# Sorted attention and routed experts on one core: tokens kept on chip and gathered by GpSimd

## The chip, the cores and the metric

The kernel runs on one core of one Trainium2 chip. Times are device microseconds (us). Five engines matter: PE (TensorE, matmuls; its weight loads are recorded as PEld and overlap it), DVE (VectorE), ACT (ScalarE), POOL (GpSimd) and SP (SyncE, which here only issues transfers); DMA moves data between DRAM and the core's memory. "Clock" is the share of TensorE's full clock that was granted in a stretch. L415 is line 415 of the kernel's file.

Every median below is of runs on the chip. A ratio is the mean time of one kernel's fast runs over that of the other's fast runs of the same rounds, so it is not quite the ratio of the medians quoted.

## The reference

```python
# q, k, v: (4, 8, 768, 64) float32; sort_net: (4, 8, 8, 8); 3072 tokens of 512; 8 experts
P = sort_net
for _ in range(5):                          # soft permutation of 8 blocks per head
    P = exp(P - rowmax(P)); P /= rowsum(P); P /= colsum(P)
k_sorted[i] = sum_j P[i, j] * k_block[j]    # blocks of 96 rows; the same for v
attn  = softmax(q_block @ k_sorted_block.T / 8)     # inside each block of 96
x     = (attn @ v_sorted_block) as (3072 tokens, 512 = 8 heads * 64)
for e in range(8):                          # each token has one expert, domain_id
    out[domain_id == e] = relu(x[domain_id == e] @ w1[e]) @ w2[e]   # w1 512x1024, w2 1024x512
```

In the data drawn here the experts get 354 to 420 tokens each.

## The kernel before

It works in three stages. The setup makes the permutation and a table from slots to tokens, which goes through DRAM in 24 scatters (they run on beside attention until 150 us). Attention runs per half of the batch: K and V are mixed over the blocks by matmuls, copied, transposed by more matmuls, copied again; q is transposed; then come scores, exponential, product with V, and a division.

```python
for n in range(12):                                   # mix over blocks
    nc.tensor.matmul(mix_ps, PTg, Ka16[:, n * 512:(n + 1) * 512], start=True, stop=True)
    nc.scalar.copy(Ks16[:, n * 512:(n + 1) * 512], mix_ps)
    # ... the same for V, copied by VectorE
for n in range(24):                                   # then transpose, 4 columns of blocks at a time
    for cc in range(4):
        nc.tensor.transpose(tps[0:64, cc * 128:(cc + 1) * 128], Ks16_v[:, c0 + cc, :], idf16)
    pcopy(n, kTs[:, c0 * 128:(c0 + 4) * 128], tps[0:64, :])
# ... the same for V; then per head:
nc.tensor.matmul(sc_ps[:, ii * 96:(ii + 1) * 96], kTs_v[:, m, :],      # kTs_v: step of 128 elements
                 qT_h_v[:, :, i0 + ii, :], start=True, stop=True)
# ...
nc.sync.dma_start(x_dram...., x_g....)                # x to DRAM, once per half of the batch
```

The experts take 512 slots each. Weights are loaded two experts deep, the rows of x are fetched from DRAM by their indices, transposed, multiplied, and the results scattered.

```python
for e in range(8):
    w1e = wpool.tile([128, 4096], FP16, tag="w1e")    # wpool: bufs=2
    # ... w2e; both loaded from GpSimd's queue
    for tcc in range(4):                              # fetch 128 rows of x
        nc.gpsimd.indirect_dma_start(X[:, tcc * 512:(tcc + 1) * 512], None, x_dram.ap(), ...)
    # ... 16 transposes of X into xT, copied
    for fc in range(8):
        for dc in range(4):
            nc.tensor.matmul(h_ps, w1e[...], xT[:, dc * 512:(dc + 1) * 512], ...)   # contiguous columns
        nc.scalar.activation(hT[:, fc * 512:(fc + 1) * 512], h_ps, func=AF.Relu)
    for tcc in range(4):
        # ... 8 matmuls into o_ps, copied to out_sb (2 buffers)
        nc.gpsimd.indirect_dma_start(out, ..., out_sb, None, ...)                    # scatter 128 rows
```

The softmax here doesn't subtract the row's maximum and nothing guards it: scores larger than these inputs give would overflow.

## Time and profile before

| | us |
|---|---|
| median before (438.42 to 439.76, 3 runs) | 438.49 |
| setup, until 31 us | 31 |
| attention, 31 to 222 | 191 |
| gap and experts, 222 to 437 | 215 |

The first view cuts the profile of the kernel before into stretches. The columns are: stretch, its length, the busy time of each engine with its instructions in brackets, the mean TensorE clock, the DMA share, and GB/s.

```profile
core 0: us, PE busy (x) PEld busy (x) DVE busy (x) ACT busy (x) POOL busy (x), PEclk, DMA share, GB/s
0.00:31.00 31.00, 1.95 (x6) 0.74 (x6) 9.89 (x62) 3.02 (x8) 5.28 (x19) 1.00 0.88 155
...
157.00:222.00 65.00, 58.38 (x368) 47.21 (x366) 27.56 (x98) 17.19 (x35) 0.00 (x0) 0.50 0.00 1
222.00:244.00 22.00, 0.58 (x2) 0.39 (x2) 0.86 (x4) 0.00 (x0) 8.86 (x10) 0.50 0.88 190
244.00:437.00 193.00, 138.48 (x640) 62.99 (x640) 16.46 (x32) 56.09 (x96) 70.29 (x71) 0.85 0.65 129
```

In 157–222, attention, PE is busy 58 of 65 us at half the clock: PE is the limit there. In 222–244 almost nothing computes. In 244–437 PE is busy for 138 of 193 us.

The second view is the list of waits of the kernel before: who waited, for what, the sum, how often, and the longest one.

```profile
DVE out_sb L42 <- DMA out_dram<-out_sb,s2tx: 92.9, 10, 11.9
...
POOL w1e L315 <- DMA x_dram<-x_g: 79.3, 1, 79.3
...
POOL out_dram L354 <- DMA out_dram<-out_sb,s2tx: 58.7, 16, 6.9
```

The one wait of 79.3 us explains the gap: the first load of weights waits until x has been written to DRAM (the pool of the weight tiles is opened only after attention's pools are closed), so no weight moves during attention. The other two are the scatters of results: only one is under way at a time, and the copies out of PSUM wait for their two buffers.

The third view is two lines of the groups of instructions of the kernel before: line, engine, operation, tiles, shapes, count, busy us, mean ns of one, idle time before them and its releaser.

```profile
L340 PE MATMUL h_ps<-xT,w1e 128*128 128x512 f16 x256 | 71.6, 444 | 2.4 <-ACT xT L44 2.0
...
L270 PE MATMUL sc_ps<-qT_h,kTs 64*96 64x96 f16 x256 | 49.2, 364 | 7.2 <-DVE qT_h L265 7.1
L270 PEld LDWEIGHTS <-kTs 64*96 64x96 f16 x256 | 44.3, 252 | 14.1 <-DVE qT_h L265 10.8
```

A score matmul is narrow (96 columns), yet its record lasts 364 ns, and that of its weight load, with a step of 128 elements, 252 ns. Records of matmuls overlap, so the mean of one is not its share of the time: 49.2 us for 256 is 192 ns each.

### The profile page before, as it was taken

The numbers are of one execution on the slowest core, as the hardware profiler recorded it, in microseconds if no ns is written. First come the engines' busy times: TensorE is split into PE (matmuls) and PEld (weight loads), VectorE is DVE, ScalarE is ACT, GpSimd is POOL, SyncE is SP. The second block draws the span as 40 slices with busy tenths as digits, with TensorE's granted clock in tenths as the row PEclk, the third lists the DMA queues.
The fourth block names the chain that finished last, engine by engine and source line by source line (L and its number), as shares of the span: only waits on it lengthen the run. The fifth ranks groups of instructions, "written<-read, shape, count | busy, mean of one in ns | idle before, by whom it ended". The sixth has DMA issues, their size and how long they took to land. (4 is left out here: it accounts for less than half of the span.)

```text
span 437.5 us, 4602 instructions
## 1 busy us (share of the span) xinstructions
PE 306.0 (70%) x1722; PEld 188.3 (43%) x1722; DVE 113.6 (26%) x367; ACT 126.7 (29%) x234; POOL 111.7 (26%) x128
## 2 busy tenths in 40 slices
PE   0109789999897389898920595959493966959680
PEld 0004476777676367676720242424241422424330
DVE  5306734454444234444420001010100001010110
ACT  2004743333225342222200232314141513323420
POOL 4001334331010100000007433426242624421211
PEclk9999955555557955555555597988898886969995
DMA  7950960000009100000049987877696876764110
GB/s 146 206 86 0 160 130 2 2 2 0 2 2 241 50 1 0 1 1 2 0 144 152 220 176 125 176 142 150 134 179 121 166 129 119 144 129 107 73 48 24
DMA packets 23921, 40.40 MB, mean 92 GB/s; under 512 B 3706, under 2 KB 15996, under 8 KB 23708
## 3 DMA queue, kind: packets, MB, share of 16 engines
q0 software_dynamic: 22688, 36.87, 44.5%
q1 hardware_dynamic: 1212, 3.26, 2.2%
q8 instruction: 13, 0.21, 0.2%
q14 instruction: 8, 0.07, 0.0%
HBM read 56.69 MB, written 11.60 MB: 156 GB/s over the span
## 5 line engine op out<-in xcount | busy, mean ns | idle before, releaser
L340 PE MATMUL h_ps<-xT,w1e 128*128 128x512 f16 x256 | 71.6, 444 | 2.4 <-ACT xT L44 2.0
L348 PE MATMUL o_ps<-w2e,hT 128*128 128x512 f16 x256 | 59.2, 387 | 4.6 <-ACT out_sb L44 4.6
L354 POOL DMA_INDIRECT out_dram<-out_sb,s2tx x32 | 32.0, 1002 | 103.8 <-DMA out_dram<-out_sb,s2tx 58.7
L270 PE MATMUL sc_ps<-qT_h,kTs 64*96 64x96 f16 x256 | 49.2, 364 | 7.2 <-DVE qT_h L265 7.1
L275 ACT ACTIVATE ET<-sc_ps 96x384 f16<-96x384 f32 x64 | 31.1, 486 | 79.4 <-PE sc_ps L270 79.4
L42 DVE COPY out_sb<-o_ps 128x512 f32<-128x512 f32 x16 | 11.1, 692 | 160.9 <-DMA out_dram<-out_sb,s2tx 92.9
L333 PE MATMUL xps<-idf_118,X 128*128 128x128 f16 x128 | 13.4, 248 | 56.3 <-DVE xT L42 34.1
L270 PEld LDWEIGHTS <-kTs 64*96 64x96 f16 x256 | 44.3, 252 | 14.1 <-DVE qT_h L265 10.8
L216 POOL DMA_INDIRECT slot2tok<-val_239,dest_i x24 | 23.9, 994 | 87.9 <-DMA slot2tok<-val_239,dest_i 53.9
L340 PEld LDWEIGHTS <-w1e 128*128 128x128 f16 x256 | 28.4, 113 | 40.3 <-issue 20.3
L344 ACT ACTIVATE hT<-h_ps 128x512 f16<-128x512 f32 x64 | 38.1, 597 | 21.9 <-PE h_ps L340 21.5
L348 PEld LDWEIGHTS <-hT 128*128 128x128 f16 x256 | 25.3, 99 | 36.8 <-issue 8.1
L279 PE MATMUL av_ps<-VsC,ET 96*96 96x65 f16 x256 | 39.7, 296 | 0.0
L321 POOL DMA_INDIRECT X<-x_dram,s2tx x32 | 32.8, 1025 | 18.6 <-issue 8.8
L333 PEld LDWEIGHTS <-X 128*128 128x128 f16 x128 | 9.7, 108 | 61.4 <-issue 36.7
L279 PEld LDWEIGHTS <-ET 96*96 96x96 f16 x256 | 30.3, 177 | 10.0 <-issue 9.2
L264 PE MATMUL qps<-idf_118,Qa_133 128*64 128x128 f16 x192 | 33.4, 313 | 0.4 <-ACT VsC L44 0.4
L44 ACT COPY xT<-xps 128x512 f16<-128x512 f16 x16 | 9.4, 586 | 79.3 <-PE xps L333 79.3
L265 DVE COPY qT_h<-qps 64x384 f16<-64x384 f16 x64 | 21.8, 341 | 33.1 <-PE sc_ps L270 30.4
L315 POOL DMA_DIRECT2D w1e<-in_moe_w_dram x8 | 6.7, 832 | 79.9 <-DMA x_dram<-x_g 79.3
L44 ACT COPY out_sb<-o_ps 128x512 f32<-128x512 f32 x16 | 9.4, 585 | 49.4 <-DMA out_dram<-out_sb,s2tx 43.7
L264 PEld LDWEIGHTS <-Qa_133 128*64 128x64 f16 x192 | 18.5, 152 | 8.7 <-issue 3.2
(276 smaller groups left out, 246.0 us busy)
## 6 DMA issues: line engine op xcount, KB each, us to landing
w1e<-in_moe_w_dram POOLq DMA_DIRECT2D x8, 1024.0 KB
w2e<-in_moe_w_dram POOLq DMA_DIRECT2D x8, 1024.0 KB
Ka_126<-in_k_dram POOLq DMA_DIRECT2D x4, 768.0 KB
Va_127<-in_v_dram POOLq DMA_DIRECT2D x4, 768.0 KB
Qa_133<-in_q_dram POOLq DMA_DIRECT2D x2, 1536.0 KB
x_dram<-x_g SPq DMA_DIRECT2D x2, 1536.0 KB
X<-x_dram,s2tx POOLq DMA_INDIRECT x32
out_dram<-out_sb,s2tx POOLq DMA_INDIRECT x32
```

Source lines behind the costliest of these rows:

```text
L216: nc.gpsimd.indirect_dma_start(slot2tok.ap(), bass.IndirectOffsetOnAxis(ap=dest_i[:, j:j + 1], axis=0), val2[:, 2 * j:2 * j + 2], None, bo ...
L264: nc.tensor.transpose(qps[0:64, t * 128:(t + 1) * 128], q16[:, (t0 + t) * 64:(t0 + t + 1) * 64], idf16)
L265: nc.vector.tensor_copy(qT_h[:, t0 * 128:(t0 + 3) * 128], qps[0:64, 0:384])
L270: nc.tensor.matmul(sc_ps[:, ii * 96:(ii + 1) * 96], kTs_v[:, m, :], qT_h_v[:, :, i0 + ii, :], start=True, stop=True)
L275: nc.scalar.activation(ET, sc_ps, func=AF.Exp, scale=0.125)
L279: nc.tensor.matmul(av_ps[:, ii * 65:(ii + 1) * 65], ET[:, ii * 96:(ii + 1) * 96], VsC_v[:, m, :], start=True, stop=True)
L321: nc.gpsimd.indirect_dma_start(X[:, tcc * 512:(tcc + 1) * 512], None, x_dram.ap(), bass.IndirectOffsetOnAxis(ap=s2tx[:, 8 * e + 2 * tcc + ...
L333: nc.tensor.transpose(xps[:, tcc * 128:(tcc + 1) * 128], X[:, tcc * 512 + dc * 128:tcc * 512 + dc * 128 + 128], idf16)
L340: nc.tensor.matmul(h_ps, w1e[:, dc * 1024 + fc * 128: dc * 1024 + fc * 128 + 128], xT[:, dc * 512:(dc + 1) * 512], start=(dc == 0), stop=( ...
L344: nc.scalar.activation(hT[:, fc * 512:(fc + 1) * 512], h_ps, func=AF.Relu)
L348: nc.tensor.matmul(o_ps, hT[:, fc * 512 + tcc * 128: fc * 512 + tcc * 128 + 128], w2e[:, fc * 512:(fc + 1) * 512], start=(fc == 0), stop=( ...
L354: nc.gpsimd.indirect_dma_start(out, bass.IndirectOffsetOnAxis(ap=s2tx[:, 8 * e + 2 * tcc:8 * e + 2 * tcc + 1], axis=0), out_sb, None, boun ...
```

## The change

The intent: one matmul both mixes and transposes a piece of K or V (its moving operand is a mask times the permutation). x never leaves the chip: it is kept transposed, with the four 128-wide chunks of one token side by side (`xT[p, token, 4]`), and GpSimd gathers the tokens of an expert from it with `indirect_copy`. An expert has 448 slots; a loop with a count read at run time takes what exceeds them, which here is nothing, so it runs zero times. Weight tiles go from two to five, and five experts' weights are loaded during attention. The 64 slots beyond 384 of two neighbouring experts share one tile ("tails"), so there are 28 scatters where there were 32. The order of instructions on PE, ACT, DVE and GpSimd is that of the program.

The diff is a rewrite; this is its core, with cuts marked.

```diff
-    P_dram, x_dram, slot2tok, cnt_rt, base_rt = ...            # four tables and x through DRAM
+    wpool = ctx.enter_context(tc.tile_pool(name="wp", bufs=5))
+    xT = keep.tile([128, NTOK, 4], FP16, tag="xT")             # x, on chip
 ...
-            nc.tensor.matmul(mix_ps, PTg, Ka16[:, n * 512:(n + 1) * 512], ...)   # mix, copy,
-            nc.tensor.transpose(tps[0:64, ...], Ks16_v[:, c0 + cc, :], idf16)    # transpose, copy
+    def interleave(p):                                          # GpSimd orders K, V, q of two heads
+        nc.gpsimd.tensor_copy(kv[:, :, 0::3, :], ks[:, h].rearrange("p h (t d) -> p t h d", d=D))
+        # ... two more
+    def kv_mm(p, lst):                                          # mixes and transposes at once
+        # ...
+            nc.tensor.matmul(o[:, s]..., kv[:, t, h], M[:, bh]..., start=True, stop=True)
 ...
-                nc.sync.dma_start(x_dram..., x_g...)
+    def x_tr(p):                                                # 8 transposes, then into xT
+        # ...
+        nc.scalar.copy(xT[:, b * 768:(b + 1) * 768, hp], o.rearrange("p i c -> p (i c)"))
 ...
+            if 6 <= p <= 14 and p % 2 == 0:
+                load_w((p - 6) // 2)                            # five experts during attention
 ...
-                nc.gpsimd.indirect_dma_start(X[...], None, x_dram.ap(), ...)      # 4 per expert
-                ... nc.tensor.transpose(xps[...], X[...], idf16) ...
+    def gather(e):
+        xg = moe.tile([128, CAP, 4], FP16, tag="xg", name="xg")
+        for s in range(2):
+            nc.gpsimd.indirect_copy(xg[:, s * 224:(s + 1) * 224, :], xT, gidx[:, e, s * 14:(s + 1) * 14], ...)
 ...
-                nc.tensor.matmul(h_ps, w1e[...], xT[:, dc * 512:(dc + 1) * 512], ...)
+                nc.tensor.matmul(h_ps, w1e[:, dc, fc * 128:(fc + 1) * 128], xg[:, :, dc], ...)  # step of 4
 ...
+        for e in range(NE):
+            if first and e >= 1 and e + 4 < NE:
+                load_w(e + 4)                                   # experts 5, 6, 7
+            ...
+            hts[e] = up(e, xg)
+            xg = gather(e + 1)
+            down(e, hts[e])                                     # 3 x (8 matmuls, copy, scatter)
+            if e % 2 == 1:
+                tails(e - 1, hts[e - 1], hts[e])
```

## The prediction

> **What bounds it now.** The table of stages (busy time per stretch) shows three stages. 0–31 us: setup, PE busy 2 us. 31–222: attention. PE is busy 58.4 of the 65 us in 157–222 at granted clock 0.50, with narrow matmuls: by groups, a score matmul is 364 ns and its strided weight load 252 ns; the timeline shows eight scores in 1.54 us. 222–437: experts. The list of waits shows one wait of 79.3 us of the first weight load on the write of x to DRAM, so weights start only then; PE idles 21.5 us for the first gathered X. In 244–437 PE is busy 138 of 193 us although 32 matmuls at full clock take 7.1 us (about 221 ns each): outputs wait for scatters (DVE 92.9 us, ACT 43.7, GpSimd 58.7). The chain of waits is nearly empty and no help.
>
> **Start, estimated 32 us.** No bounce of tables through 24 scatters; but the new mask products and one-hot tables stand on DVE ahead of the first K/V copies.
>
> **Attention, estimated 98 us (now 191).** Mixing and transposing become one matmul; 640 separate mixing/transposing matmuls and their copies, and 64-to-96-column strided weight loads, go. Per pair of heads DVE now has, costed by like shapes in the trace: 512-element fp32 copy 0.68, half of it 0.42, 768-element copy about 0.55, two V copies 0.84, four reciprocals and products 2.35: 4.85 us. ACT: 0.59+0.39+4×0.49+0.79 = 3.7. PE: 74 matmuls, about 4 us at full clock, 5.5–6 at half. So about 6 us, DVE-bound, PE near it, times 16, plus the last transpose: attention ends near 130 us. Weights of five experts load meanwhile.
>
> **Experts, estimated 190 us (now 215).** PE needs only 12–13 us per expert at full clock. The new limit is GpSimd, one in-order queue. Each expert has two gathers of 224 entries. No such instruction is in this trace. [...] Scatters still wait for each other (the order of instructions shows each waiting for the previous one's semaphore): 1.0 us issue plus about 2.5 us landing in the trace: 28 cost about 75 us of that same queue. Also, the load of the sixth and eighth expert's second weights waits for the 64-row tails of the pair before, ahead of the next gather: some 10 us. Thus about 200 us; I shade this to 190 as gathers may be quicker.
>
> **Total 320 us**, 80% range 258–360. Faster by over 2%: 0.96; within 2%: 0.015; slower: 0.025.
>
> **Right or wrong in the profile.** Right: gathers 5–7 us each; GpSimd busy or waiting for scatters almost throughout the expert stage; PE idle before the up matmuls, released by GpSimd; PE busy about 100 us there; gaps largest at experts 3 and 5; attention about 6 us per pair with DVE over 75% busy; the first weights landed before attention ends. Wrong: gathers near 1–2 us make experts PE-bound, about 115 us, total near 245; pairs of 7–8 us mean that in-order waits, or GpSimd's interleaving copies, bind attention.
>
> **What would make it wrong.** The gather's time above all: each microsecond moves the total by 16. [...] Then: scatters landing slower next to weight loads; [...] a PE clock staying at half in attention; strided moving operands from the gathered x.

The sum for the experts came to about 200 us, shaded to 190, and the total to 320; the 75 us of scatters and the 10 us of waits do not make up the 200. The gather of 5–7 us is the author's estimate. PE's figures are estimates too. The numbers of the kernel before to set beside them: 32 matmuls of 512 columns take 7.07 us at a clock of 1.00 (from 255.57 us), and a transpose of 128 columns adds 58 ns at 1.00 (L248: four in 0.38 us, eight in 0.61) and 108 ns at 0.50 (L254: 0.58 and 1.01).

## The result, and the profile after

The kernel after takes 400.25 us (median of 4 runs, 399.19 to 400.75), against 439.12 us (4 runs, 438.42 to 440.33) of the kernel before in the same rounds; the ratio is 0.9107, with a 95% interval of 0.9081 to 0.9134. It is faster, as predicted, but 80 us slower than the predicted 320 and outside the range of 258 to 360.

The stretches of the kernel after, with the same columns as above (38 is the start of the first scores, 136 the end of attention's matmuls, 153 the first up matmul of the first expert):

```profile
0.00:38.00 38.00, 5.91 (x74) 5.42 (x76) 32.84 (x87) 3.52 (x8) 24.16 (x39) 1.00 1.08 158
38.00:136.00 98.00, 79.05 (x1153) 68.49 (x1147) 69.67 (x210) 68.16 (x110) 38.94 (x49) 0.62 0.89 145
136.00:153.00 17.00, 0.00 (x0) 0.10 (x1) 0.00 (x0) 0.37 (x1) 1.75 (x2) 0.50 0.00 0
153.00:399.00 246.00, 151.33 (x512) 52.13 (x511) 19.37 (x28) 34.84 (x64) 50.92 (x49) 0.81 0.23 52
```

| stage | before, us | predicted, us | after, us |
|---|---|---|---|
| start | 31 | 32 | 38 |
| attention | 191 | 98 | 98 |
| experts to the end | 215 | 190 | 263 |

So attention gave back the 93 us that it should, and the experts took 48 us more than before instead of 25 us less. In the expert stage no engine looks busy: PE 151 of 246 us, GpSimd 51, the DMA share 0.23. Something serial that the busy times do not show must bound it.

Three groups of the kernel after:

```profile
L415 PE MATMUL h_ps<-xg,w1e 128*128 128x448 f16 x256 | 102.6, 574 | 98.7 <-POOL xg L405 98.7
...
L405 POOL INDIRECT_COPY xg<-xT,gidx 128x896 f16 x16 | 19.2, 1203 | 143.7 <-issue 143.7
...
L431 PE MATMUL o_ps<-w2e,hT 128*128 128x512 f16 x192 | 42.9, 380 | 0.0
```

The gather seems cheap, 1203 ns each. But GpSimd is idle 143.7 us before the sixteen gathers, put down to "issue", that is, to nothing that the profile shows; and PE waits 98.7 us for them. GpSimd's timeline of the kernel after shows why (start, length, engine, line, operation, count, and in brackets the idle time before it with its releaser):

```profile
143.91 1.19 POOL L405 INDIRECT_COPY xg<-xT,gidx 128x896 f16 x1 [33.48 <-issue]
152.44 1.19 POOL L405 INDIRECT_COPY xg<-xT,gidx 128x896 f16 x1 [7.34 <-issue]
160.96 1.19 POOL L405 INDIRECT_COPY xg<-xT,gidx 128x896 f16 x1 [7.32 <-issue]
169.47 1.19 POOL L405 INDIRECT_COPY xg<-xT,gidx 128x896 f16 x1 [7.32 <-issue]
170.85 1.12 POOL L423 DMA_INDIRECT out_dram<-o_sb,sidx  x1 [0.19 <-DVE o_sb L422]
174.51 1.02 POOL L423 DMA_INDIRECT out_dram<-o_sb,sidx  x1 [2.54 <-issue]
178.07 0.97 POOL L423 DMA_INDIRECT out_dram<-o_sb,sidx  x1 [2.54 <-issue]
179.04 0.84 POOL L355 DMA_DIRECT2D w1e<-in_moe_w_dram  x1
191.69 0.93 POOL L356 DMA_DIRECT2D w2e<-in_moe_w_dram  x1 [11.81 <-PE o_ps L438]
200.01 1.22 POOL L405 INDIRECT_COPY xg<-xT,gidx 128x896 f16 x1 [7.39 <-issue]
```

Gathers that follow each other start 8.51 to 8.53 us apart. The second one's record ends at 152.44 + 1.19 = 153.63, and PE's first up matmul starts at 153.69; after a load of weights that ends at 192.62 the next gather's record ends at 201.23, 8.61 us later. So a gather takes about 8.5 us and only its last 1.2 us is recorded; the "idle" time is the gather at work. This is how the trace reads, 1.2 us recorded and 8.5 us of spacing; half_entries below tests it.

The same lines show the rest of the queue: 2.5 us between two scatters, and a wait of 11.81 us in front of the second load of expert 5, for matmuls of L438, which are the tails. The list of waits of the kernel after has it twice:

```profile
POOL w2e L356 <- PE o_ps L438: 22.8, 2, 11.8
```

And PE's timeline of the kernel after shows the up matmuls:

```profile
153.69 12.83 PE L415 MATMUL h_ps<-xg,w1e 128*128 128x448 f16 x32 [19.21 <-POOL xg L405]
166.34 5.36 PE L431 MATMUL o_ps<-w2e,hT 128*128 128x512 f16 x24
```

Thirty-two up matmuls of 448 columns take 12.83 us, 401 ns each; 24 down matmuls of 512 columns take 5.36 us, 223 ns each (the 574 and 380 ns of the groups are records that overlap). The narrower one is nearly twice as slow. The difference between the two is how the moving operand lies: `xg[:, :, dc]` has a step of 4 elements (8 bytes), `w2e[:, fc]` is contiguous. All eight up stages take 12.83 us, while the mean clock in them lies between 0.78 and 1.00.

Summed over GpSimd's timeline, from 136.6 us (the end of the first gather, 145.10, less 8.53) to the end at 398.7:

| what stands in GpSimd's queue | us |
|---|---|
| 16 gathers of 8.53 | 136.5 |
| scatters of experts 0 to 6, each waiting for the one before | 71.3 |
| waits of the sixth and eighth experts' loads for the tails | 22.8 |
| issuing loads | 5.3 |
| expert 7 after its gather: matmuls, four scatters, the end (less the scatters of expert 6) | 26 |
| sum | 262 |

The sum is the length of the stage, 262 us. That is a reading, not yet a test.

### The profile page after: what moved, and what is told of

The parts are those of the page before. It is cut to its first block, busy times and chain, and to the rows that moved or that the text cites. A ratio compares the mean times of both kernels' runs of the same rounds, so it can differ in the third digit from the quotient of the medians.

```text
span 398.7 us, 4513 instructions
## 1 busy us (share of the span) xinstructions
PE 236.3 (59%) x1732; PEld 126.1 (32%) x1732; DVE 121.9 (31%) x324; ACT 106.9 (27%) x182; POOL 115.8 (29%) x138
## 5 line engine op out<-in xcount | busy, mean ns | idle before, releaser
L415 PE MATMUL h_ps<-xg,w1e 128*128 128x448 f16 x256 | 102.6, 574 | 98.7 <-POOL xg L405 98.7
L417 ACT ACTIVATE hT<-h_ps 128x448 f16<-128x448 f32 x64 | 34.8, 544 | 206.9 <-PE h_ps L415 206.9
L422 DVE COPY o_sb<-o_ps 128x512 f32<-128x512 f32 x28 | 19.4, 692 | 232.0 <-PE o_ps L431 227.3
L405 POOL INDIRECT_COPY xg<-xT,gidx 128x896 f16 x16 | 19.2, 1203 | 143.7 <-issue 143.7
L423 POOL DMA_INDIRECT out_dram<-o_sb,sidx x28 | 28.1, 1005 | 62.5 <-DMA out_dram<-o_sb,sidx 28.8
L348 ACT COPY xT<-x_ps 128x768 f16<-128x768 f16 x16 | 29.9, 1867 | 10.5 <-PE x_ps L347 10.3
L340 DVE TENSOR_TENSOR xr<-av_ps,rc 96x256 f16<-96x256 f32 x64 | 26.9, 421 | 2.2
L277 PE MATMUL kv_ps<-M,kvx 128*128 128x128 f16 x192 | 24.2, 291 | 4.9 <-DVE M L125 4.9
L277 PEld LDWEIGHTS <-kvx 128*128 128x128 f16 x192 | 17.3, 132 | 6.8 <-issue 4.9
L356 POOL DMA_DIRECT2D w2e<-in_moe_w_dram x8 | 7.3, 908 | 22.8 <-PE o_ps L438 22.8
L313 PE MATMUL v_ps<-idf_86,kvT_301 64*128 64x64 f16 x128 | 8.5, 221 | 7.4 <-ACT xT L348 7.4
L313 PE MATMUL v_ps<-idf_86,kvT_302 64*128 64x64 f16 x128 | 8.1, 219 | 7.6 <-ACT xT L348 7.6
```

The lines of the kernel that those rows point to most:

```text
L277: nc.tensor.matmul(o[:, s].rearrange("p i c -> p (i c)"), kv[:, t, h], M[:, bh].rearrange("p i c -> p (i c)"), start=True, stop=True)
L313: nc.tensor.transpose(o[:, i], kt[r, c0:c0 + 128], idf16[r, r])
L340: nc.vector.tensor_tensor(xr[p][:, 4 * ih:4 * ih + 4, h * D:(h + 1) * D], o[0:BLK, :, 0:D], rc.unsqueeze(2).to_broadcast([BLK, 4, D]), op= ...
L348: nc.scalar.copy(xT[:, b * 768:(b + 1) * 768, hp], o.rearrange("p i c -> p (i c)"))
L405: nc.gpsimd.indirect_copy(xg[:, s * 224:(s + 1) * 224, :], xT, gidx[:, e, s * 14:(s + 1) * 14], i_know_this_is_slow=True)
L415: nc.tensor.matmul(h_ps, w1e[:, dc, fc * 128:(fc + 1) * 128], xg[:, :, dc], start=(dc == 0), stop=(dc == 3))
```

## The experiments

The main theory, A: GpSimd's in-order queue bounds the expert stage, and its largest term is the gather, which costs by entry. Rivals: B, the gather costs by the bytes that it moves; C, PE bounds the stage, because the up matmuls run at half speed, and the gathers lie mostly under them; D, the scatters' landing or the loads that wait for the tails are the cause, and the gathers matter little. Each run below is an edit of the kernel after; five of the kernels are correct, and the others give a wrong result, as marked. Several were with the kernel before on the same chip; the ratios are to that kernel. One caution: edits of the expert stage alone also moved the start of the first gather, between 133.7 and 137.2 us (136.6 in the kernel after), for a reason that no run shows. So 2 or 3 us of any difference below may not come from the edit.

### half_entries: half the entries per gather

Wrong result: 111 of 224 entries are gathered, into two tiles that were zeroed once.

```diff
-            nc.gpsimd.indirect_copy(xg[:, s * 224:(s + 1) * 224, :], xT, ...)
+            nc.gpsimd.indirect_copy(xg[:, s * 224:s * 224 + 111, :], xT, ...)
```

> Wrong result on purpose: each gather fetches 111 entries in place of 224; everything else as in the changed kernel. Theory (the gather really takes the 8.5 us between starts, in proportion to its entries): the spacing of two gathers back to back falls to about 4.3 us; the GpSimd queue loses 16 x 4.2 = 67 us, PE becomes the limit, total 310 to 335 us. Rival (the 7.3 us of idle time before each gather record is a fixed cost of each instruction, or a wait): spacing stays near 8.5 us and the total near 400.

Measured: 340.92 us (2 runs), ratio 0.774 (0.770 to 0.778). GpSimd's timeline:

```profile
137.86 0.81 POOL L409 INDIRECT_COPY xg<-xT,gidx 128x444 f16 x1 [28.26 <-issue]
142.21 0.81 POOL L409 INDIRECT_COPY xg<-xT,gidx 128x444 f16 x1 [3.54 <-issue]
```

The spacing falls to 4.34 us, by 4.19 us for 113 entries: 37 ns per entry, which leaves about 0.2 us fixed. Removing 16 × 4.19 = 67 us from the queue removed 59 us from the kernel. The total lies a little above the expected 310 to 335, because the matmuls and their tails start to be waited for (the waits for tails are still 23.4 us). Theory A stands; C in its pure form falls, since PE's work is unchanged.

### half_elements: same entries, half the bytes

Wrong result: 224 entries of 2 elements.

```diff
-            nc.gpsimd.indirect_copy(xg[:, s * 224:(s + 1) * 224, :], xT, ...)
+            nc.gpsimd.indirect_copy(xg[:, s * 224:(s + 1) * 224, 0:2],
+                                    xT.rearrange("p n (a b) -> p (n a) b", b=2), ...)
```

> Wrong result on purpose: each gather fetches 224 entries of 2 elements in place of 4. [...] the spacing stays at 7.5 to 8.5 us and the total at 385 to 400. Rival (cost by bytes or elements): spacing 4.3 to 5 us, total below 340.

Measured: 385.12 us (2 runs), ratio 0.8744 (0.8709 to 0.8779).

```profile
151.02 0.89 POOL L409 INDIRECT_COPY xg<-xT,gidx 128x448 f16 x1 [6.50 <-issue]
158.35 0.95 POOL L409 INDIRECT_COPY xg<-xT,gidx 128x448 f16 x1 [6.45 <-issue]
```

The spacing is 7.33 us, a little under the expected 7.5 to 8.5: half the bytes save 1.2 of 8.53 us, half the entries save 4.2. (7.5 to 8.5 us was expected if the bytes hardly count.) Theory B falls: most of the cost goes with the entries.

### no_gather: no gathers at all

Wrong result: the up matmuls read 448 neighbouring tokens of xT, with the same step of 8 bytes.

```diff
-        xg = moe.tile(...); ... nc.gpsimd.indirect_copy(...) x2 ...; return xg
+        return xT
 ...
-                nc.tensor.matmul(h_ps, w1e[...], xg[:, :, dc], ...)
+                nc.tensor.matmul(h_ps, w1e[...], xg[:, 374 * e:374 * e + CAP, dc], ...)
```

> Wrong result on purpose: no gathers; the up matmuls read 448 neighbouring tokens of x on chip, at the same 8-byte step. Theory (queue-bound): the queue keeps about 100 us of scatters, PE needs 8 x 18.1 + 4 x 1.8 = 152 us and becomes the limit; no 17 us before the first matmul; total 290 to 305 us. Rival (scatters, not gathers, hold the stage): total above 350.

Measured: 300.67 us (2 runs), ratio 0.6826 (0.6803 to 0.685), as expected. Without gathers the kernel would run 100 us faster; then PE is busy 147 of the 148 us from 134 to 282, and its matmuls set the time:

```profile
134.71 12.83 PE L411 MATMUL h_ps<-xT,w1e 128*128 128x448 f16 x32 [1.94 <-ACT xT L348]
147.36 5.36 PE L427 MATMUL o_ps<-w2e,hT 128*128 128x512 f16 x24
152.56 12.82 PE L411 MATMUL h_ps<-xT,w1e 128*128 128x448 f16 x32
```

Thirty-two up matmuls still take 12.83 us with no gather running, so their slowness does not come from GpSimd working beside them.

### dense_moving: the up matmul reads contiguous columns

Wrong result.

```diff
-                nc.tensor.matmul(h_ps, w1e[...], xg[:, :, dc], ...)
+                nc.tensor.matmul(h_ps, w1e[...], xg.rearrange("p n d -> p (n d)")[:, 448 * dc:448 * dc + 448], ...)
```

> Wrong result on purpose: the up matmuls read their 448 moving columns side by side in place of every fourth element; the gathers are unchanged. Theory (the 8-byte step of the moving operand is what makes an up matmul cost 401 ns): spacing falls to about 190 ns at full clock, up stage of an expert from 12.8 to 6.1 us. Since the GpSimd queue is the limit, only the stretches where it waits for PE get shorter (two waits for the tails, the last expert): total 375 to 385. Rival (PE is the limit of the expert stage): 8 x 6.7 = 54 us less, total near 346. If the matmul stays at 400 ns, the cause is not the step.

Measured: 380.13 us (2 runs), ratio 0.8631 (0.8569 to 0.8692), as expected.

```profile
167.84 5.84 PE L415 MATMUL h_ps<-xg,w1e 128*128 128x448 f16 x30 [3.14 <-POOL xg L405]
```

The group of all up matmuls in this run:

```profile
L415 PE MATMUL h_ps<-xg,w1e 128*128 128x448 f16 x256 | 68.6, 436 | 112.7 <-POOL xg L405 112.7
```

In the first of these views, the second expert's, the clock was 90% or more (PEclk 9 in both slices of the page that it touches); thirty take 5.84 us, at most 195 ns each. An estimate from the 223 ns of a down matmul of 512 columns, scaled to 448, is 195 ns too. In the other seven experts thirty take 7.3 to 8.4 us. There PE had waited 7.6 us for a gather just before, and 3.14 us in the view; and where such a stretch fills over 80% of a slice of the page (the first, third and fifth expert), PEclk is 7, that is 70 to 79%. So over the stage the up matmuls take 68.6 us rather than 102.6, a third less and not half. The kernel gains 20 us of these 34, and PE still waits 112.7 us for gathers: PE is not the limit. The kernel gains through the queue, since the loads wait 10.3 us for the tails rather than 22.8, and through the last expert (22.0 us after its gather rather than 25.9).

### stride2_moving: a step of 4 bytes

Wrong result on purpose; a single look, so its state is unknown.

```diff
+   ... xg.rearrange("p n d -> p (n d)")[:, 896 * (dc // 2) + dc % 2:896 * (dc // 2) + 896:2], ...
```

> Wrong result on purpose: the up matmuls read their 448 moving columns at a step of 2 elements (4 bytes) in place of 4 elements (8 bytes). With side-by-side columns a matmul cost 190 ns at full clock, at 8 bytes 401 ns. If PE pays for bytes passed over, the 4-byte step lies at 190 to 215 ns (nothing to pay up to some step) or near 270 to 300 ns (in proportion). [...] a value near 400 ns would mean that any step at all halves the rate.

Measured: 379.18 us (1 run).

```profile
168.05 6.09 PE L415 MATMUL h_ps<-xg,w1e 128*128 128x448 f16 x30 [3.12 <-POOL xg L405]
```

Thirty take 6.09 us at a clock of 90% or more (PEclk 9 in both slices of the page), about 200 ns each. So a step of 4 bytes costs about 200 ns against at most 195 for contiguous columns, and a step of 8 bytes 401 ns (the second expert of the kernel after, at a clock of 1.00). At a lower clock the gap is smaller: the 401 ns stayed the same at mean clocks from 0.78 to 1.00, while a contiguous matmul took 277 ns where PEclk was 7 (30 in 8.31 us, the first expert of dense_moving).

### chunk_major: pay for the order in the gather instead

A correct kernel: the gather writes the four elements of an entry 896 bytes apart, so that the matmul reads contiguous columns.

```diff
-        xg = moe.tile([128, CAP, 4], FP16, tag="xg", name="xg")
+        xg = moe.tile([128, 4, CAP], FP16, tag="xg", name="xg")
 ...
-            nc.gpsimd.indirect_copy(xg[:, s * 224:(s + 1) * 224, :], xT, ...)
+            nc.gpsimd.indirect_copy(xg[:, :, s * 224:(s + 1) * 224].rearrange("p d n -> p n d"), xT, ...)
```

> Correct kernel. Each gather writes its four elements per entry 896 bytes apart, so that the up matmuls read their columns side by side. If the gather still takes 8.5 us: matmul at about 190 ns and total 375 to 385, like the run with dense columns and a wrong result. If the spread write slows the gather: each microsecond adds 16 us.

Measured: 432.93 us (4 runs, 432.22 to 436.23), ratio 0.9852 (0.9789 to 0.9915), which counts as unclear against the kernel before.

```profile
140.83 4.42 POOL L405 INDIRECT_COPY xg<-xT,gidx 128x896 f16 x1 [32.02 <-issue]
152.23 4.42 POOL L405 INDIRECT_COPY xg<-xT,gidx 128x896 f16 x1 [6.98 <-issue]
```

The spacing rises to 11.4 us, by 2.9 us for each gather: 46 us for sixteen. The faster matmuls (32 in 8.65 us, the third expert's, and not 12.83) return part of it, but the kernel is 33 us slower than the kernel after. A faster PE does not pay for a slower GpSimd here. That is theory A again, tried in the other direction.

### loads_late: the loads behind the tails they wait for

A correct kernel: the loads of experts 5 to 7 move from the start of an iteration to its end, where the tails that free the tile have already been issued and their scatter stands in front.

```diff
-            if first and e >= 1 and e + 4 < NE:
-                load_w(e + 4)                      # ahead of the gather of e + 1
 ...
+            if first and e >= 1 and e + 4 < NE:
+                load_w(e + 4)                      # after down(e) and the tails
```

> Correct kernel. Only the place of the loads of experts 5 to 7 in the queue is changed: behind the scatters and tails in place of ahead of the gather. The two waits of 11.8 and 11.0 us for the tails go. Theory: total 376 to 384 us. If the waits come back elsewhere: 390 to 400.

Measured: 375.86 us (4 runs, 375.6 to 377.51), ratio 0.855 (0.8508 to 0.8593), at the lower edge of the expected range. The waits of 11.81 and 11.01 us are gone and the kernel is 24 us faster; from the start of the first gather to the end it is 22.1 us. So these two waits, 22.8 us, stand on the critical path nearly in full; part D is right as a part, but only 24 us of it.

### scatter_apart: scatters that need not wait for each other

Wrong result: the scatters go in turn to `out` and three spare tensors.

```diff
+    outs = [out] + [three spare tensors of the same shape]
-        nc.gpsimd.indirect_dma_start(out, ...)
+        nc.gpsimd.indirect_dma_start(outs[len(put_n) % 4], ...)
```

> Wrong result on purpose: scatters go in turn to the output and to three spare tensors, so that none waits for the previous one to land. Theory (about 20 waits of 2.5 us in the queue, on its critical path): total 350 to 362 us, with PE the nearer limit. Rival (the waits are covered): above 385.

Measured: 366.72 us (2 runs), ratio 0.8332 (0.8286 to 0.8379); a little above the expected range.

```profile
170.55 1.01 POOL L428 DMA_INDIRECT spare<-o_sb,sidx  x1 [0.30 <-issue]
...
189.98 0.92 POOL L356 DMA_DIRECT2D w2e<-in_moe_w_dram  x1 [16.30 <-PE o_ps L443]
```

Between two scatters GpSimd now waits 0.30 us rather than 2.5, so the wait was for the scatter before to the same tensor. The scatters of experts 0 to 6 take 30.6 us of the queue rather than 71.3. But GpSimd then reaches the load sooner and waits longer for the tails: 16.30 and 15.49 us, where it was 11.81 and 11.01. So nine of the 41 us removed come back as a longer wait in the same queue, more than the 5 us of the miss.

### as_costed: the two wrong terms set to what the prediction assumed

Wrong result: 168 entries per gather, and contiguous columns for the up matmul, together.

```diff
-            nc.gpsimd.indirect_copy(xg[:, s * 224:(s + 1) * 224, :], xT, ...)
+            nc.gpsimd.indirect_copy(xg[:, s * 224:s * 224 + 168, :], xT, ...)
 ...
-                nc.tensor.matmul(h_ps, w1e[...], xg[:, :, dc], ...)
+                nc.tensor.matmul(h_ps, w1e[...], xg.rearrange("p n d -> p (n d)")[:, 448 * dc:448 * dc + 448], ...)
```

> Wrong result on purpose. This puts the prediction's two mis-sized terms to what the prediction had assumed, at once: 168 entries per gather (at 38 ns an entry 6.4 us, the predicted gather) and an up matmul that reads contiguous columns (about 190 ns, the predicted matmul). Nothing else changes. If the two terms, together with a start 6 us later and the 10 us shaded off, are the whole of the error of 80 us, this must come to 330 to 348 us, and the waits of the sixth and eighth experts' loads for the tails to 5 to 8 us each. If the parts do not add up (the gather alone gives 6.4/8.53 of the way, about 366; the matmul alone gave 380), and something else stands in the expert stage, it stays above 352.

Measured: 348.96 us (4 runs, 346.52 to 350.3), ratio 0.7971 (0.7948 to 0.7995): one microsecond above the expected range, and below the 352 that would have spoken for another cause.

```profile
146.49 1.00 POOL L409 INDIRECT_COPY xg<-xT,gidx 128x672 f16 x1 [5.44 <-issue]
152.91 1.00 POOL L409 INDIRECT_COPY xg<-xT,gidx 128x672 f16 x1 [5.42 <-issue]
...
174.88 0.92 POOL L356 DMA_DIRECT2D w2e<-in_moe_w_dram  x1 [5.37 <-PE o_ps L443]
```

The gathers are 6.42 us apart, within the predicted 5–7 us ("the predicted gather" of the expectation is the author's estimate; 6.4 us is 168 entries at 8.53 / 224 = 0.038 us), and the waits for the tails are 5.37 and 5.55 us, about the "some 10" of the prediction. So the two terms alone are worth 400.25 − 348.96 = 51 of the 80 us. The matmul is only in part the predicted one: in the second expert, where PE has not waited, 32 up matmuls take 6.22 us (PEclk 9), but in the others, where PE waits 5.5 to 5.9 us for a gather before the last thirty, these take 7.26 to 8.78 us (PEclk 5, 7 and 8 in the three slices of the page that such a stretch fills by over 80%), and on average an expert's take 68.9 / 8 = 8.6 us. GpSimd's queue from 134.6 us to the end at 344.7 now sums to 102.9 (gathers) + 69.2 (scatters of experts 0 to 6) + 10.9 (tails) + 5.3 (issue) + 21.4 (the last expert) = 210 us, where the prediction had "about 200", shaded to 190.

### x_by_dram, x_by_dram_2, x_by_dram_3: the old way to fetch x, in the new kernel

All three are correct kernels. They keep the new attention and early weights, but write x to DRAM per pair of heads and fetch rows by indirect DMA, as the kernel before did (28 fetches, then transposes on PE). The transposed columns are contiguous, so the up matmuls are fast too (32 in 6.22 us, the second expert of x_by_dram_2). They use six weight tiles, and the last two experts' loads stand behind the tails, as in loads_late. So they differ from the kernel after by more than x's way, and what they gain is not the price of the gather alone.

```diff
-        nc.scalar.copy(xT[:, b * 768:(b + 1) * 768, hp], ...)           # and its 8 transposes
+        nc.sync.dma_start(x_dram....rearrange("(i c) e -> c i e", c=BLK), xr[p])
 ...
-            nc.gpsimd.indirect_copy(...)                                  # 2 per expert
+            row_gather(X[:, m], 3 * e + m)                                # 3 or 4 per expert, a DMA each
+    def turn(e, X):  # 16 transposes of X and Xt on PE, copied by DVE and ACT into xg[128, 4, CAP]
```

First version:

> Correct kernel. Undoes one part of the change, x on chip with gathers by GpSimd: each pair's x goes to DRAM from SyncE, rows come back by indirect DMA (28 of 128 rows) and PE transposes them; attention loses its x transposes and the 1.87 us copies; six experts' weights fit. Estimate for the queue: 28 fetches at 1.3 us, 28 scatters at about 3.5 us, weights 6: about 140 us; attention ends near 132. Theory (the gathers' 136 us made the stage long): total 270 to 290 us. Rival (x through DRAM costs what the kernel before paid): above 330.

Measured: 321.85 us (4 runs, 321.01 to 323.24), ratio 0.7307 (0.7274 to 0.734). Faster than both kernels, but the expectation missed by 32 us: x's writes land late (a median of 15.2 us after their issue, with the weight loads under way), and attention waits for its x buffers.

```profile
DVE xr L339 <- DMA x_dram<-xr: 34.7, 9, 19.0
```

The first fetch was issued at 159.1 us. The second version issues the writes from ACT's queue with six buffers, loads four experts' weights in attention, and weaves the fetches of expert e + 2 between the scatters of e:

```diff
-        nc.sync.dma_start(x_dram..., xr[p])        # xr: bufs=3
+        nc.scalar.dma_start(x_dram..., xr[p])      # one pair later, xr: bufs=6
 ...
             put(o_ps, 3 * e + m)
+            row_gather(X[:, m], 3 * (e + 2) + m)
```

> Correct kernel. The version with x through DRAM, mended where its profile showed new waits: x is written from ACT's queue a pair later with six buffers (in place of SyncE, which was held by small table transfers, and three), only four experts' weights are loaded during attention (in place of six, behind which the writes of x stood), fetches are put between the scatters, so that the queue has work while a scatter lands. Theory (those waits, 30 to 40 us in all, were its excess over my estimate): total 250 to 280 us. If DMA traffic as a whole is its limit: no better than 300.

Measured: 318.64 us (4 runs, 316.06 to 320.37), ratio 0.7269 (0.7234 to 0.7304): another miss. The first fetch came at 129.0 us, 30 us sooner, but the stage from there to the end grew from 162 to 185 us:

```profile
PE xtr L427 <- DMA X<-x_dram,gidx: 44.0, 14, 11.3
```

The fetches stand behind scatters, and in this run scatters that follow a load of weights in the same queue land late (GpSimd waited 9.29 and 10.24 us behind two of them, and about 1.2 us behind most others). The third version puts the fetches ahead of the scatters again and loads five experts in attention:

> Correct result. As the second version of x through DRAM, with the fetch of expert e+2 ahead of the scatters of expert e again (as in the first version), five experts loaded in attention, and the sixth after the first fetches. If the fetches that stood behind the scatters were what cost the second version its gain, PE's wait for X falls from 44 us to under 25 and the total to 285 to 305 us. If the scatters that land late behind weight loads bound it, the total stays at 312 to 322.

Measured: 302.43 us (4 runs, 301.08 to 303.9), ratio 0.6889 (0.6868 to 0.6911), within the expected range. Three of its stretches:

```profile
38.00:118.00 80.00, 59.51 (x1028) 48.62 (x1025) 66.07 (x210) 38.62 (x94) 38.89 (x49) 0.80 1.03 165
118.00:145.00 27.00, 0.09 (x2) 0.09 (x1) 0.71 (x3) 0.00 (x0) 2.99 (x3) 0.50 0.95 163
145.00:302.00 157.00, 121.79 (x640) 58.01 (x640) 24.36 (x36) 42.08 (x72) 59.05 (x60) 0.86 0.43 103
```

In its list of waits PE still waits 38.9 us for X, so the other half of the expectation, under 25 us, missed. Of this, 26.9 us is one piece before the first expert, while the DMA engines are 0.95 busy; all later waits for X sum to 12 us. So the second version seems to have lost by its order of fetches, scatters and loads; the third changed the order of fetches and the number of early experts together, and does not separate the two. This is the fastest correct kernel, by 31% against the kernel before and by about a quarter against the kernel after (0.6889 / 0.9107 = 0.756). The nearest correct kernel with x on chip is loads_late, at 375.86 us.

## Why the prediction was right or wrong

**Right: faster, and attention.** Attention was predicted at 98 us and takes 98 (38 to 136). DVE's costs, taken from like shapes of the kernel before, held: 690, 415 and 421 + 171 ns for what was costed at 0.68, 0.42 and 2.35 / 4. But attention is not DVE-bound, as the text said: DVE is busy 69.7 of 98 us (71%, below the 75% that it named) and PE 79 at a clock of 0.62. ACT was mis-costed: the copy into xT takes 1.87 us and not 0.79. That the sum came out right is therefore partly luck: the prediction had rounded 4.85 us of DVE per pair up to 6, and the room was filled by something else. The last versions of x through DRAM show by what, as far as the record goes. They take x's transposes off PE and the copies into xT off ACT, and x_by_dram_3's attention takes 80 us (38 to 118) rather than 98, or 5.0 us per pair, with DVE busy 83% of it. PE's wait list in the kernel after agrees: 15.0 us, in 14 waits, of the V transposes for that copy on ACT. These versions change other things beside, so this is not an experiment on attention alone.

**Right: what bounds the expert stage.** GpSimd's queue, with gathers, scatters that wait for one another, and loads that wait for the tails. The runs with half the entries, with no gathers, with late loads and with scatters apart each moved the total by what they took from that queue, less what came back as another wait (with no gathers, PE became the limit first); taking 34 us from PE's up matmuls moved it by only 20 us, and making PE faster at GpSimd's cost (chunk_major) made the kernel slower.

**Wrong, first: "gathers 5–7 us each".** A gather takes 8.53 us, 136.5 us for sixteen; at the 6.42 us of as_costed it would be 102.9: 34 us of the error. The time of a gather was the author's estimate, and what it was worked out from no trace or run here shows. The runs show 38 to 39 ns per entry (8.53 us for 224, 6.42 for 168, 4.34 for 111), and 1.2 us more for four elements than for two. So the cost goes mostly by entry and less by byte, and a gather of 6.42 us is a quarter too small.

**Wrong, second: "PE needs only 12–13 us per expert at full clock".** An up stage takes 12.83 us and not about 6.2 (32 contiguous ones in 6.22 us, as_costed), so an expert takes about 19 us of PE. Nor was the full clock to be had: with contiguous columns and PE waiting for gathers, an up stage takes 8.6 us on average (as_costed, with the clock given there). That the gathered x would be read with a step was only a last item in the prediction's list of what might go wrong. It does not make PE the limit, but the load of weights in GpSimd's queue waits for the tails, which come after the up matmuls: "some 10 us" became 22.8. The last expert, which nothing overlaps, grew too. Together with the gathers this is 51 us, as the run with both terms set back shows. The runs of one term each give nearly the same: 20 us for the matmuls, and an estimated 34 for the gathers (8.53 − 6.42 us, by sixteen).

**Wrong, third: "I shade this to 190 as gathers may be quicker".** This took 10 us off for a hope; they were slower.

**Wrong, fourth: the smaller terms.** The first scores start at 37.8 us and not at 32, since DVE is busy for 32.8 of the first 38 us; attention therefore ends about 6 us late. And GpSimd's queue, "about 200" in the prediction, is 210 us even with a gather of 6.42 us: the wait for the last expert and the end were sized by feel. The 29 us that as_costed leaves (348.96 − 320) are accounted for by its profile: the first gather starts at 134.6 us and not 130 (4.6), the queue takes 210.1 us and not 190 (20.1, with the 10 us of the shade in it), the time of a run is 1.8 us more than the span of its profile, and the profiled run was 2.4 us faster than the median.

So where did the expected gain go? Into a stage that the change had moved from the DMA engines to one in-order queue. Fetching x from DRAM had cost GpSimd about 1 us of issue for 128 rows; gathering on chip costs it 8.5 us for 224, in the same queue that must issue scatters and loads. Together with the copies into xT, keeping x on chip was a loss here, as far as the runs can say: the third version of x through DRAM, with most of the rest of the change, needs 302 us, and the best correct kernel with x on chip 376.

## What to carry to other kernels

Before moving work onto an engine that also issues transfers, add up that engine's queue in order, with every wait in it, and measure the one instruction that the trace does not have: here a single gather of two sizes would have shown an estimated 34 of the 80 us by which the prediction was off. Time such an instruction by the spacing of starts, since its recorded length can hide most of it (here 1.2 us were recorded of 8.53). And when a layout is chosen for one engine, such as four chunks side by side for a gather, look at the step in bytes that the next engine, here PE, then has to read with (401 ns at 8 bytes, at most 195 contiguous).
